# A build-time list scheduler: due times from cumulative TensorE time, SBUF merges counted on a shared port, accumulating transfers assumed to land later

## The chip, the cores and the metric

The kernel runs on one core of a Trainium2 chip. The metric is the device time of one execution in microseconds (us); the number to compare is the median of several executions. A core has five engines that the text names as the profile does: PE (TensorE, matrix products; PEld is its weight load), DVE (VectorE), ACT (ScalarE), POOL (GpSimd) and SP (SyncE, which here only issues transfers). SBUF is the on-chip working memory, PSUM the small memory that PE writes its products to, in banks.

## The reference

An attention block without softmax feeds a mixture of four experts, all in float32:

```python
# q, k, v: (8 batches, 8 heads, 576, 64)
kv  = einsum('bhsd,bhse->bhde', k, v)
out = einsum('bhsd,bhde->bhse', q, kv)
out = out / sqrt(mean(out * out, axis=-1) + 1e-6) * g_norm
x   = out as (4608, 512)                       # N x D
p   = domain_probs / (domain_probs.sum(-1) + 1e-9)
y   = 0
for e in range(4):                             # w1[e]: 512 x 1024, w2[e]: 1024 x 512
    y += p[:, e] * (maximum(x @ w1[e], 0) @ w2[e])
```

## The kernel before

**Tiling.** The 4608 rows of x are nine chunks of 512: one per batch, and a ninth that collects the last 64 rows of every batch. There are 36 steps, s = 9 e + c for expert e and chunk c. A step's `up` makes the hidden layer (x @ w1, ReLU), and its `down` multiplies by w2 and adds the result into the output in DRAM. Both replace eight block products by seven (the scheme of Strassen in the form of Winograd), in `up` on two levels. That saves PE time and adds many sums and differences of blocks in SBUF, which go through `combine` (line 371) and may run on DVE or on POOL, whichever is free.

**Three kinds of steps.** Step 0 has plain products in `up_plain`. Steps 1 to 7 are "mixed": the batch's attention, the two-level `up`, and a `down` with five one-level products per half plus one group, (4, 2), on two levels in `down_deep`. Steps 8 to 34 are "deep": two-level `up` and `down_deep` with four groups. Step 35 is a one-level `down`. The weights of expert e+1 are loaded, and their sums formed, while steps 8, 17 and 26 run: these are the three hand-overs. At a hand-over some forms are made by `subtract_from`: ACT copies a block with the sign turned (line 432), then a transfer from POOL's queue adds DRAM data into it (line 438).

**Merging.** `result` gives each step two accumulators (`acc`, of kind `big`) and the functions `merge` and `send`. `merge` scales by the probability and writes or adds into the accumulator. The first one into a cell is an ACT copy with scale (line 1130). The others are `scalar_tensor_tensor` on DVE (line 1137). In the one-level `down` a merge reads PSUM; in `down_deep` it reads SBUF, where the products have been put together. So in the mixed steps 1 to 7 four merges per step read SBUF on DVE, 28 in all; in the deep steps all SBUF merges are fresh and run on ACT. `send` writes the accumulator out. For expert 0 and at the last step it is a plain transfer from SP's queue (line 1155), otherwise an accumulating transfer from POOL's queue (line 1153). The accumulator's buffer is free when the transfer has landed.

**The order is planned when the kernel is built.** Every operation is added to a `Plan` with a key (its step plus a fraction), a cost by engine, and its dependencies. `Plan.layout` is a list scheduler: it walks through simulated time, and an engine that is free picks an operation which is ready by the plan's clock, within a reach of keys (0.7 for PE, 0.9 for DVE, ACT and POOL). PE and SP take the first ready one in key order. DVE, ACT and POOL take the ready one with the earliest due time. The engines' instruction streams are then issued in the planned order, and each instruction waits for semaphores where its data are not there. The plan also picks the buffers (31 of kind `big`, and two more once the attention is over), so a plan that thinks a buffer free too early makes an instruction wait at the head of its engine's queue.

**Due times.** An operation's own due time is its key times `STEP` (44 us), plus `LATE` (20 us) if it does not run on PE. Going backwards, each operation's due time is then lowered to that of every operation that needs it, less its own cost and a gap of 0.06 or 0.3 us. So `LATE` counts only for operations that lead to no PE work.

**The port.** Operations with `port=True` exclude each other in the plan: `combine` and `add` set it. When the program is written out, a POOL operation with the flag also gets a real dependency on the last such DVE operation before it in the order.

**Landing.** An operation with `kb` that is not on SP is an accumulating transfer: its cost of 1.0 us is followed by 9.0 us for 512 KB and 5.5 us for anything smaller (the sends) until its buffer counts as free, and 0.3 us more.

Of the kernel before, what the change touches and what calls it, by code (L numbers as in the profile page):

```python
# [2 lines left out]

# [31 lines left out]
class Plan:  # L35
# [13 lines left out]

    SPARE = {"big": 6, "small": 3, "xf": 3}  # L50
    FORMS = 9.0
    STEP, LATE = 44.0, 20.0
    SLOW = 6.8

    def __init__(self):
# [27 lines left out]
    def layout(self, slots, later, idle, idle_banks, idle_until):  # L83
# [9 lines left out]
        todo = {e: [] for e in self.REACH}  # L93
# [3 lines left out]
                todo[e].append(op)  # L97
        for e in todo:
            todo[e].sort(key=lambda o: (o.key, o.n))
        for op in self.ops:  # L100
            op.due = op.key * self.STEP + (0.0 if "PE" in op.cost else self.LATE)
        for op in reversed(self.ops):
            for d in op.deps:
                cross = self.SAME if op.cost.keys() == d.cost.keys() else self.CROSS
# [2 lines left out]
        bus, port = 3.8, 0.0  # L107
# [28 lines left out]
        while left:  # L136
# [4 lines left out]
            for eng in todo:  # L141
                if busy[eng] > t:
                    continue
                pending = todo[eng]
                while pending and pending[0].start is not None:
                    pending.pop(0)
                if not pending:
                    continue
                reach = pending[0].key + self.REACH[eng]
                best = None  # L150
                for op in pending:
                    if op.key > reach:
                        break
                    if op.start is not None:
                        continue
                    if best is not None and op.due >= best.due:
                        continue
                    when = ready(op, eng)
                    if when is None:
                        continue  # L160
                    if when > t:
                        heapq.heappush(wake, when)
                        continue
                    best = op
                    if eng in ("PE", "SP"):
                        break
                if best is not None:
                    op = best
                    op.start, op.eng = t, eng
                    if eng == "SP":  # L170
                        busy[eng] = t + op.cost[eng]
                        bus = max(bus, t + 1.5) + op.kb / 215.0
                        op.end = bus + 0.5
                        lanes = lanes[1:] + [op.end]
                    else:
                        op.end = busy[eng] = t + op.cost[eng]
                        if op.kb:
                            op.end += 9.0 if op.kb == 512 else 5.5
                    if op.port:
                        port = op.end  # L180
                        heapq.heappush(wake, port)
                    for b in op.outs:
                        if b.kind is not None and b.slot is None:
                            free[b.kind].sort()
                            b.slot = free[b.kind].pop(0)[1]
                            b.ap = slots[b.kind][b.slot]
                    for b in op.bufs:
                        b.left -= 1
                        if b.left == 0 and b.kind is not None:
                            end = max(o.end for o in [op] + b.readers + b.writers) + self.CROSS  # L190
                            free[b.kind].append((end, b.slot))
                            live[b.kind] -= 1
                            ended[b.kind] = max(end, ended.get(b.kind, 0.0))
                            for rule in [r for r in later if not any(live.get(k) for k in r[0])]:
                                later.remove(rule)
                                end = max(ended[k] for k in rule[0])
                                for ap in rule[2]:
                                    free.setdefault(rule[1], []).append((end, len(slots[rule[1]])))
                                    slots[rule[1]].append(ap)
                                heapq.heappush(wake, end)  # L200
                    heapq.heappush(wake, busy[eng])
                    heapq.heappush(wake, op.end + self.SAME)
                    heapq.heappush(wake, op.end + self.CROSS)
                    order.append(op)
                    left -= 1
                    moved = True
                if eng == "PE" and busy[eng] <= t and 1.6 <= t and front < idle_until:
                    kind, spare = next((
                        (k, f) for k in idle_banks for f in free[k] if f[0] <= t
                    ), (None, None))  # L210
                    if spare is not None:
                        took = 0.43 if t < self.SLOW else 0.23
                        op = Op(front, {"PE": took}, None, (), (), 0, False)
                        op.start, op.eng, op.end = t, eng, t + took
                        op.fn = lambda eng, bank=slots[kind][spare[1]]: idle(bank)
                        busy[eng] = op.end
                        free[kind].remove(spare)
                        free[kind].append((op.end, spare[1]))
                        heapq.heappush(wake, op.end)
                        order.append(op)  # L220
                        moved = True
# [13 lines left out]
def kernel(  # L235
# [105 lines left out]
    def pe(products, columns, passes=2):  # L341
        return {"PE": passes * products * (0.0025 + columns / 1200.0) + 0.003}
# [745 lines left out]
    def result(s, e, c, base):  # L1088
# [6 lines left out]
        acc = [Buf("big", f"acc{s}_{j}") for j in range(2)]  # L1095
# [12 lines left out]
        def cell(i, half=None):  # L1108
            at = (i % 2) * DM
            if half is None:  # L1110
                return acc[i // 2].ap[:, at:at + DM]
            return acc[i // 2].ap[:, at + half * HN:at + (half + 1) * HN]
# [6 lines left out]
                        128, reads=[summed[c, i]], also=[part[i, 0], part[i, 1]],  # L1119
                    )  # L1120

        def merge(key, src, ap, i, half, fresh):

            def prob():
                return p_all[:, c * NR + i, e:e + 1]

            if fresh and not again:
                plan.add(
                    key, {"ACT": 0.48},
                    lambda eng: nc.scalar.activation(  # L1130
                        out=cell(i, half), in_=ap(), func=ACT.Copy, scale=prob()),
                    reads=[probs] + src, parts=[acc[i // 2]], writes=[part[i, half]],
                )
            else:
                plan.add(
                    key, {"DVE": 0.5},
                    lambda eng: nc.vector.scalar_tensor_tensor(  # L1137
                        out=cell(i, half), in0=ap(), scalar=prob(), in1=cell(i, half),
                        op0=ALU.mult, op1=ALU.add,
                    ),  # L1140
                    reads=[probs, part[i, half]] + src, parts=[part[i, half]],
                    holds=[acc[i // 2]],
                )

        def send(key, i):
# [15 lines left out]
            )  # L1161

        return merge, send

    def down(s, e, c, mixed=False):
# [47 lines left out]
    def down_deep(s, e, c, groups=((1, 6), (7, 5), (4, 2), (3,)), base=None, h=None, merge=None, send=None):  # L1213
# [5 lines left out]
        if not mixed:  # L1219
            h = hidden.pop(s)  # L1220
            base = s + 1.2
            merge, send = result(s, e, c, base)
        prods, half = {}, {}
        for i, group in enumerate(groups):
            n = len(group)
            at = base + 2 * i / 7
# [32 lines left out]
            for j, mm in enumerate(ORDER):  # L1259
                key = at + n * j / 49  # L1260
                ps = bank[{2: 2, 5: 5, 3: 5}.get(mm, 1)]

                def product(eng, group=group, mm=mm, ps=ps, forms=forms):
# [11 lines left out]
                op = plan.add(  # L1275
                    key, pe(2 * n, P), product,
                    reads=[b for m in group for b in (w2q[e][m][mm][0], forms[m][mm][0])]
                    + ([ps] if mm == 2 else []),
                    **{"parts" if mm == 2 else "writes": [ps]},
                    after=(inner_last[-2:-1] or primed) if mm == 1 else seeds if mm == 5 else (),  # L1280
                )
# [43 lines left out]
            key = at + n / 7  # L1325

            def whole(m):
                pair, o = prods[m]
                return pair.ap[:, o * NT:(o + 1) * NT]
# [10 lines left out]
            def out_(m, th, dh):  # L1340

                for b in range(2):
                    merge(
                        key - 0.2, [half[m], prods[m][0]],
                        lambda b=b: whole(m)[:, b * HN:(b + 1) * HN], 2 * th + b, dh, not mixed,
                    )

            if mixed:
# [133 lines left out]
```

## Time and profile before

| | us |
|---|---|
| median of 4 runs | 1691.43 |
| lowest and highest of them | 1689.82, 1693.16 |
| the profiled execution, whole | 1693.94 |
| its span, first to last instruction | 1692.2 |
| PE busy in the span | 1678.5 (99%) |
| DVE, ACT, POOL busy | 1252.6 (74%), 985.0 (58%), 733.2 (43%) |
| mean granted PE clock | 0.999 |

A group of instructions is named by line, engine, operation and the tiles it writes and reads; `big<-big,p_all` means that a `big` buffer is written from a `big` buffer and the probabilities. "q" after an engine's name is its queue or sequencer: SPq L377 is a transfer issued from SP. "A <- B: 2.6, 1, 2.6" in the view of waits says that A's engine stood still until B had ended: total us, times, longest. A busy PE counts from the first to the last of its pipelined matmuls, so a half-speed clock shows as busy.

### The profile page before, as it was taken

Reading aid. Unit: us, or ns where it says so; the run is one execution under the profiler, and the core shown is the slowest. Engines: PE = TensorE matmul, PEld = TensorE weight load, DVE = VectorE, ACT = ScalarE, POOL = GpSimd, SP = SyncE. Lnnn points to the kernel's source line nnn. Section 1 sums busy time; section 2 is a strip of 40 time slices with the busy share of each in tenths; the row PEclk is TensorE's granted clock in tenths of the full one; section 3 lists DMA queues with packets and bytes.
Section 4 is the critical chain, followed back from the end, with each engine's and each line's share of the span. In section 5 each row is a group of like instructions: output and inputs, shape, how many; then the busy total and the mean of one; then the engine's idle time right before and its main releaser. Section 6 shows DMA issues by size and latency. Waiting matters only on the chain.

```text
span 1692.2 us, 66409 instructions
## 1 busy us (share of the span) xinstructions
PE 1678.5 (99%) x29030; PEld 1574.1 (93%) x29030; DVE 1252.6 (74%) x2054; ACT 985.0 (58%) x2405; POOL 733.2 (43%) x663
## 2 busy tenths in 40 slices
PE   9999999999999999999999999999999999999998
PEld 6687888888889999999999999999999999999996
DVE  4965675576788678777777887878778877787874
ACT  3454555555455666666665666666666666666662
POOL 3723343434453464333365455334356554343432
PEclk9999999999999999999999999999999999999999
DMA  9865553643556344535477444444478544444442
GB/s 241 227 209 152 174 164 103 183 154 121 185 156 150 114 115 105 121 105 120 132 191 174 114 114 114 114 108 113 110 190 203 123 114 114 114 114 110 119 102 51
DMA packets 172331, 234.27 MB, mean 138 GB/s; under 512 B 61577, under 2 KB 112649, under 8 KB 172041
## 3 DMA queue, kind: packets, MB, share of 16 engines
q1 hardware_dynamic: 148968, 193.32, 37.2%
q0 software_dynamic: 23072, 36.71, 14.8%
q8 instruction: 228, 3.74, 0.9%
q14 instruction: 63, 0.51, 0.1%
HBM read 155.79 MB, written 74.19 MB: 136 GB/s over the span
## 4 chain that ended last, share of the span: by engine, by line
PE 94%; DVE 2%; POOL 1%; DMA 1%; issue 0%; SPq 0%; ACT 0%; ACTq 0%; POOLq 0%; DVEq 0%
PE u L348 44%; PE db L348 31%; PE ab L348 14%; PE ab L708 1%; PE ab L753 1%; PE ab L685 1%; PE ab L735 1%; DVE big L1137 1%; DMA out_dram<-big 1%; POOL rt L593 1%; DVE big L371 1%; DMA small<-in_q_dram 0%; DVE tot L400 0%; POOL xf L371 0%; PE ab L797 0%
## 5 line engine op out<-in xcount | busy, mean ns | idle before, releaser
L371 DVE TENSOR_TENSOR big<-big,big 128x1024 f32<-128x1024 f32 (+1 forms) x524 | 489.3, 949 | 31.8 <-ACT big L951 11.7
L348 PE MATMUL u<-xf,big 128*64 128x128 f32 x6784 | 487.2, 273 | 2.9 <-ACT snap L987 2.8
L348 PEld LDWEIGHTS u<-xf,big 128*64 128x64 f32 x6784 | 393.4, 137 | 8.2 <-ACT snap L987 3.8
L348 PE MATMUL u<-xf,w1y 128*64 128x128 f32 x5304 | 391.8, 273 | 2.1 <-DVE big L995 1.5
L348 PE MATMUL db<-big,big 128*64 128x128 f32 (+1 forms) x4336 | 365.9, 307 | 0.4 <-DVE big L602 0.3
L995 DVE TENSOR_TENSOR big<-u,snap 128x256 f32<-128x256 f32 x464 | 195.0, 421 | 227.8 <-PE u L348 175.7
L371 POOL TENSOR_TENSOR big<-big,big 128x256 f32<-128x256 f32 (+1 forms) x194 | 251.9, 1305 | 257.9 <-DVE big L371 131.4
L348 PEld LDWEIGHTS u<-xf,w1y 128*64 128x64 f32 x5304 | 309.2, 137 | 7.1 <-DVE big L995 1.7
L348 PEld LDWEIGHTS db<-big,big 128*64 128x64 f32 x4336 | 267.0, 137 | 39.4 <-DVE big L602 0.5
L987 ACT ACTIVATE snap<-u 128x256 f32<-128x256 f32 x490 | 188.3, 384 | 168.5 <-PE u L348 131.8
L987 ACT ACTIVATE big<-u 128x256 f32<-128x256 f32 x464 | 178.5, 385 | 103.5 <-PE u L348 80.3
L371 POOL TENSOR_TENSOR big<-big 128x512 f32<-128x512 f32 (+1 forms) x82 | 103.5, 1264 | 120.6 <-DVE big L371 73.6
L1296 ACT ACTIVATE snap<-db 128x256 f32<-128x256 f32 (+1 forms) x230 | 82.7, 359 | 114.4 <-PE db L348 105.5
L951 ACT ACTIVATE big<-big 128x1024 f32<-128x1024 f32 x131 | 137.8, 1052 | 6.3 <-DVE big L371 3.4
L371 DVE TENSOR_TENSOR big<-big 128x512 f32<-128x512 f32 (+1 forms) x130 | 117.5, 911 | 0.5 <-POOL w1y L371 0.5
L1304 DVE TENSOR_TENSOR big<-ab,snap 128x256 f32<-128x256 f32 x170 | 71.7, 422 | 58.9 <-ACT snap L1296 31.0
L987 ACT ACTIVATE u<-u 128x256 f32<-128x256 f32 x245 | 90.8, 371 | 32.4 <-PE u L348 17.7
L1153 POOL DMA_DIRECT2D out_dram<-big x108 | 96.5, 1027 | 27.1 <-ACT big L1130 23.9
L1334 POOL TENSOR_TENSOR big<-big 128x512 f32<-128x512 f32 x24 | 31.2, 1299 | 172.0 <-DVE big L371 170.8
L1130 ACT ACTIVATE big<-big,p_all 128x256 f32<-128x256 f32 x206 | 97.9, 500 | 5.7 <-POOL big L1334 5.3
L348 PE MATMUL db<-kv,big 128*64 128x128 f32 x1360 | 99.1, 273 | 0.0
L348 PE MATMUL ab<-big,big 128*64 128x128 f32 (+1 forms) x1360 | 96.7, 278 | 0.0
(183 smaller groups left out, 2406.9 us busy)
## 6 DMA issues: line engine op xcount, KB each, us to landing
xf<-x SPq DMA_DIRECT2D x108, 512.0 KB, 4.0
out_dram<-big POOLq DMA_DIRECT2D x92, 256.0 KB, 6.4
xf<-x_h SPq DMA_DIRECT2D x81, 256.0 KB, 3.4
xf<-x SPq DMA_DIRECT2D x81, 256.0 KB, 3.9
x<-xf SPq DMA_DIRECT2D x36, 512.0 KB, 4.8
big<-in_moe_w_dram SPq DMA_DIRECT2D x31, 512.0 KB, 5.6
x_h<-big SPq DMA_DIRECT2D x18, 512.0 KB, 4.5
small<-in_q_dram SPq DMA_DIRECT2D x64, 128.0 KB, 4.2
```

Source lines behind the costliest of these rows:

```text
L348: nc.tensor.matmul(out_[cols], lhsT=lhsT[:, cols], rhs=rhs, **kw)
L371: lambda eng: adder(eng).tensor_tensor(out=out_(), in0=a(), in1=b(), op=op),
L593: nc.gpsimd.tensor_tensor(out=rt.ap[0:n, 0:2 * blocks], in0=ss.ap[0:n, 0:2 * blocks], in1=mhalf[0:n, 0:2 * blocks], op=ALU.pow,)
L685: nc.tensor.transpose(bank.ap[:, rs], qt.ap[:, rs], ident[:])
L951: lambda eng: nc.scalar.activation(out=b.ap[:], in_=b.ap[:], func=ACT.Relu),
L987: lambda eng: nc.scalar.activation(out=where(), in_=ps.ap[:, 0:HN], func=ACT.Copy),
L995: lambda eng: nc.vector.tensor_tensor(out=block(whole, a, t), in0=src.ap[:, 0:HN], in1=add_.ap[:], op=ALU.add),
L1130: lambda eng: nc.scalar.activation(out=cell(i, half), in_=ap(), func=ACT.Copy, scale=prob()),
L1153: nc.gpsimd.dma_start(out=dst, in_=cell(i)[parts, :], accum_op=ALU.add)
L1296: lambda eng: nc.scalar.activation(out=where(), in_=group_of(ps.ap), func=ACT.Copy),
L1304: lambda eng: nc.vector.tensor_tensor(out=cell(tq, dq), in0=group_of(src.ap), in1=group_of(add_.ap), op=ALU.add,),
L1334: lambda eng: adder(eng).tensor_tensor(out=whole(to), in0=whole(a), in1=whole(b), op=ALU.add),
```

## The change

Three things change in the plan's model, and nothing in what the kernel computes. First, an operation's due time is no longer its key times 44 us but the sum of the planned PE costs of all PE operations with a smaller key; `LATE` goes from 20 to 30 us. Second, an accumulating transfer that is not of 512 KB counts 8.0 us instead of 5.5 us after its issue cost. Third, the merges of `down_deep` that run on DVE and read SBUF carry the port flag.

```diff
-    STEP, LATE = 44.0, 20.0
+    STEP, LATE = 44.0, 30.0
...
+        keys, begun, spent = [], [], 0.0
+        for op in todo["PE"]:
+            keys.append(op.key)
+            begun.append(spent)
+            spent += op.cost["PE"]
+        begun.append(spent)
         for op in self.ops:
-            op.due = op.key * self.STEP + (0.0 if "PE" in op.cost else self.LATE)
+            at = begun[bisect.bisect_left(keys, op.key)]
+            op.due = at + (0.0 if "PE" in op.cost else self.LATE)
...
                         if op.kb:
-                            op.end += 9.0 if op.kb == 512 else 5.5
+                            op.end += 9.0 if op.kb == 512 else 8.0
...
-        def merge(key, src, ap, i, half, fresh):
+        def merge(key, src, ap, i, half, fresh, from_sbuf=False):
...
-                    holds=[acc[i // 2]],
+                    holds=[acc[i // 2]], port=from_sbuf,
...
                     merge(
                         key - 0.2, [half[m], prods[m][0]],
                         lambda b=b: whole(m)[:, b * HN:(b + 1) * HN], 2 * th + b, dh, not mixed,
+                        True,
                     )
```

The list `todo["PE"]` is sorted by key at that point.

More of the change, by code (lines that the diff above doesn't have):

```diff
@@ L1 @@
+import bisect
 import heapq
```

## The prediction

> **What bounds the kernel now.** I read the page's first section, then a table of windows cut where PE's busy time changes, then what PE waited for, and then the chain of waits and the timeline at the few places that had a wait. A change of order cannot make PE's products cheaper; it can only remove or add time in which PE has nothing ready. So the first question is how much of that there is. The columns of the window table are the length, then busy us (and instructions) of PE, PEld, DVE, ACT and POOL, then clock, DMA share and GB/s.
>
> ```profile
> PE 1678.5 (99%) x29030; PEld 1574.1 (93%) x29030; DVE 1252.6 (74%) x2054; ACT 985.0 (58%) x2405; POOL 733.2 (43%) x663
> ```
>
> ```profile
> 0.00:94.00 94.00, 90.66 (x1274) 60.04 (x1278) 61.49 (x116) 39.93 (x93) 46.66 (x46) 1.00 0.92 249
> 94.00:423.00 329.00, 328.76 (x5265) 276.08 (x5258) 210.51 (x376) 174.15 (x398) 123.31 (x99) 1.00 0.50 151
> 423.00:517.00 94.00, 92.24 (x1423) 81.92 (x1421) 72.82 (x122) 47.63 (x113) 41.88 (x45) 1.00 0.54 171
> 517.00:846.00 329.00, 329.00 (x6030) 328.85 (x6028) 254.72 (x406) 206.48 (x518) 143.56 (x128) 1.00 0.47 119
> 846.00:987.00 141.00, 137.64 (x2479) 136.66 (x2477) 109.03 (x197) 88.26 (x219) 78.33 (x70) 0.99 0.63 154
> 987.00:1269.00 282.00, 282.00 (x5172) 282.00 (x5170) 221.86 (x334) 177.88 (x442) 121.12 (x113) 1.00 0.51 124
> 1269.00:1410.00 141.00, 140.71 (x2564) 139.52 (x2562) 114.27 (x196) 89.36 (x222) 79.62 (x71) 1.00 0.57 140
> 1410.00:1645.00 235.00, 235.00 (x4311) 235.00 (x4307) 185.01 (x277) 146.64 (x371) 90.27 (x87) 1.00 0.48 116
> ```
>
> PE's idle time is 1692.2 - 1678.5 = 13.7 us. The windows place it: 3.34 at the start, 0.24 in the mixed steps, 1.76, 3.36 and 0.29 at the three hand-overs of weights, nothing in the three long deep stretches, and the rest (1645 to the end, 47.20 - 42.47 = 4.73) at the tail, behind the last product. The only prize in the middle is 5.65 us, and what the clock adds to it.
>
> The waits of PE name the two stalls worth having, and the chain at 897 to 911 and the timeline at 502 to 508 say what they hang on.
>
> ```profile
> PE u L348 <- ACT snap L987: 2.8, 2, 2.3
> PE u L348 <- DVE big L995: 1.7, 2, 1.5
> ```
>
> ```profile
> 897.48 11.34 DMA out_dram<-big
> 908.82 0.03 ACTq L432
> ...
> 909.86 0.38 ACT snap L987
> 910.23 0.04 issue
> 910.27 1.09 PE u L348 x8
> ```
>
> An accumulating send left at 897.48 and landed 11.34 us later. ACT's copy at L432 was to overwrite that accumulator and stood at the head of ACT's queue for 2.60 us; the small copies of products (L987) were queued behind it, and PE, whose next product needed one, stood for 2.27 us. The clock paid as well:
>
> ```profile
> 908.00:910.30 2.30, 0.03 (x3) 0.03 (x2) 2.08 (x5) 1.41 (x3) 0.24 (x2) 1.00 1.13 177
> 910.30:913.70 3.40, 3.40 (x32) 3.40 (x34) 0.42 (x1) 1.24 (x4) 2.74 (x3) 0.51 1.08 236
> ```
>
> After the stall PE ran 3.40 us at a clock of 0.51, which loses 3.40 x 0.49 = 1.7 us. The stall's price is 2.27 + 1.7 = 3.97 us.
>
> ```profile
> 502.67 5.05 DVE L1137 SCALAR_TENSOR_TENSOR big<-big,p_all,big 128x256 f32<-128x256 f32 x4
> 504.49 2.54 POOL L371 TENSOR_TENSOR big<-big,big 128x1024 f32<-128x1024 f32 x1
> 508.10 1.09 PE L348 MATMUL u<-xf,w1y 128*64 128x128 f32 x16 [1.46 <-DVE big L995]
> ```
>
> ```profile
> L1137 DVE SCALAR_TENSOR_TENSOR big<-db,p_all,big x38: 472/484/487, 82.4 to 1678.9; 128x256 f32<-128x256 f32 x38
> L1137 DVE SCALAR_TENSOR_TENSOR big<-big,p_all,big x28: 471/832/2589, 187.9 to 507.2; 128x256 f32<-128x256 f32 x28
> ```
>
> Four merges from SBUF ran beside POOL's sums and took 5.05 us together; the sum at L995 that PE needed came behind them on DVE, and PE stood for 1.46 us. The two rows of L1137 (ns, minimum/median/maximum) show the cause: the 38 merges that read PSUM never take over 487 ns, the 28 that read SBUF have a median of 832 and reach 2589. Four such merges at 457.26 took 3.90 us and led the same way to a stall of 0.26 us at 463.70.
>
> **Part 1, merges on the port.** It adds no instruction. POOL operations planned behind a merge gain a wait for it; queued behind that on POOL are other sums and, in the mixed steps, no sends (they are SP's). By the rows, 28 merges take 28.8 us and would take 28 x 0.484 = 13.6 us apart from POOL, so DVE gets back up to 15 us. It is busy 64% of the mixed stretch, so most of that is cover and counts nothing. What reaches the end is 1.46 + 0.26 = 1.72 us. The bounds are 0 (the plan puts another operation late) and 1.96 (a stall of 0.24 us at 312.6, which also has four merges upstream, goes too). I take 1.72, since both stalls hang directly on these merges. The Trainium skill, "SBUF — State Buffer", section "Who interferes with whom", says that a DVE operation with two SBUF inputs and a POOL operation that reads SBUF lock each other out for a whole instruction. That speaks against the change: keeping the two apart would free no engine time in sum, so by it this term would be 0 unless DVE has PSUM work ready meanwhile.
>
> **Part 2, sends land later.** Of the 112 sends from POOL, 48 land later than the old 1.0 + 5.5 = 6.5 us after their start, but only 2 later than the new 9.0. The send that hurt is one of these two, at 11.34. A buffer is planned free 2.5 us later, so ACT's copy would be placed 2.5 us later against a wait of 2.60: 0.1 us is left, and the stall goes with its clock loss, 3.97 us. The bounds are 0 (the copy keeps its place in the order) and 3.97. I take 3.97, since the shift is nearly the whole wait. In the Trainium skill, "TensorE: Matmul & The Clock Gate", section "Why this matters for your kernels", only idle gaps over about 3 us are said to drop the clock. A gap of 2.27 us did it here; by the rule the term would be 2.27.
>
> **Part 3, due times.** By the kernel's `pe` costs a deep step is 49 x 0.44 + 21 x 0.876 + 7 x 0.44 = 43.0 us, against a `STEP` of 44. So in the deep steps the new due times rank operations as the old ones did. A mixed step is 21.5 + 10 x 1.73 + 7 x 0.876 + 10.4 of attention = 55.3 us, and at the start two units of key hold some 19 us of PE work where 88 were counted; there the order of DVE, ACT and POOL changes. The mixed stretch idles 0.24 us in 329, so nothing can be won there. The start idles 3.34, of which 1.35 come before the first product: the bounds are a gain of 2.0 and, with no row for a worse start, a loss of the same 2.0. I take 0.
>
> `LATE` from 20 to 30 moves what leads to no PE work up to 10 us back: in the deep steps the sums of L1334, ACT's merges at L1130 (0.50 us each) and the sends behind them. No DMA changes queue; 26.0 of POOL's waits are sends behind ACT's merges, and the sums queued behind a send on POOL wait with it. Accumulators and product buffers are held that much longer. In the long deep stretches the cover is complete (0 idle). At the hand-overs it isn't: besides the copy at 908.89, two weight loads of SP waited 4.9 us in all for sends to land. A gain is bounded by the stalls that remain (0.48 at 933.1, 0.56 at 977.3, 0.23 at 1320), but there PE waits for copies of products (L987) behind ReLUs and other copies on ACT, all of which lead to PE work, so `LATE` doesn't touch them and I exclude it. The loss is between 0 and one more stall like that at 908, 3.97. I take 1.7: one like the stall at 506.65, and a small one of 0.24.
>
> **The sum.** Against the profiled execution: 1693.94 - 1.72 - 3.97 + 1.7 = 1689.95, 4.0 less. That execution lies 2.51 above the median of the runs, so the median goes to 1691.43 - 4.0 = 1687.4. A change of 0.2%, 3.4 us, is about what a measurement of this kernel can tell from none.
>
> **The rivals.**
>
> *A, stalls removed (my forecast).* For it: both stalls hang on exactly what the plan had wrong. Own range 1683.5 to 1688.0. The lower end takes all of 1.96 + 3.97 with nothing given back (1685.5) and 2.0 from the start. Chance 0.46.
>
> *B, the stalls move.* The send of 11.34 us outlasts the new 9.0 too; if the copy keeps its place the 3.97 stay, and 1.72 - 1.7 leaves 0. Or a wait at 908 goes and one like it comes at another hand-over. Time: 1691.4, or 1688.0 to 1694.8 as a band. For it: after the start PE idles in only eight places, and any new order of DVE, ACT and POOL draws those places anew. Chance 0.28.
>
> *C, slower: the hand-overs starve.* With accumulators planned busy 2.5 us longer and merges up to 10 us later, the buffers for the next expert's weights come free later, and ACT's copies and the loads that fill them wait at the heads of their queues. At 908 the copy waited 2.60 and PE lost 2.27, so only some 0.3 us of slack stood between: whatever a weight form loses beyond that, PE loses, and each time over 2 us the clock's 1.7 comes on top. Two such stalls at 3.97, less the 1.72 of the merges: +6.2, 1697.6. It decides as soon as two of the 48 weight buffers that the hand-overs fill (16 for each of three experts) come over 0.3 us late. Against it: at the third hand-over, with the same work, the whole loss was 0.29 us, so there is room. Chance 0.26.
>
> **How the numbers follow.** Faster 0.46 from A. Same 0.28 from B. Slower 0.26 from C. The range leaves out the top of C and the very bottom of A: 1683.5 to 1697.5.
>
> **What would show it.** In the changed profile the SBUF row of L1137 should have a median near 484 and a maximum under 1 us. No ACT copy at L432 should wait for `out_dram<-big`, the clock should have no dip near 0.5 after the start, and PE's idle time should be near 13.7 - 1.7 - 2.3 + 1.7 = 11.4 us. In the deep steps L1130 and L1334 should run later, with SP's waits for sends at the hand-overs a little longer. A PE idle time over 17 us, gathered in the 100 us behind a hand-over, would make the forecast wrong and C right; a PE idle time of 13 to 14 in new places is B; an idle time that drops only in the first 94 us would mean that I had the wrong part.

## The result, and the profile after

The changed kernel takes 1688.27 us (median of 34 runs) beside 1691.95 us (52 runs of before): a ratio of 0.9978, 95% interval 0.9973 to 0.9983, or 3.7 us less. The forecast was 4.0 us less. The profiled execution went from 1693.94 to 1689.92 us, its span from 1692.2 to 1687.9 us. A few executions that took far longer than the others of their kernel are left out of every ratio.

PE is busy for as long as before, and what changed is its idle time: 13.7 us before, 9.3 us after. The change adds eight lines above the functions that run here, so line 348 is now 356, 371 is 379, 432 is 440, 987 is 995, 1130 is 1138, 1137 is 1145 and 1153 is 1161. First the page's lines, then the table of windows, cut as before:

```profile
span 1687.9 us, 66495 instructions
PE 1678.6 (99%) x29038; PEld 1573.3 (93%) x29038; DVE 1240.2 (73%) x2045; ACT 977.2 (58%) x2405; POOL 716.1 (42%) x672
```

```profile
0.00:94.00 94.00, 90.52 (x1204) 60.07 (x1206) 60.30 (x116) 38.76 (x90) 42.13 (x49) 0.98 0.90 250
94.00:423.00 329.00, 329.00 (x5286) 273.75 (x5282) 202.99 (x368) 172.46 (x397) 111.11 (x96) 1.00 0.48 146
423.00:517.00 94.00, 93.98 (x1456) 83.82 (x1454) 71.76 (x133) 48.24 (x115) 40.24 (x40) 1.00 0.59 183
517.00:846.00 329.00, 328.00 (x6008) 327.58 (x6006) 256.56 (x400) 203.58 (x513) 137.60 (x130) 1.00 0.48 120
846.00:987.00 141.00, 140.97 (x2582) 140.64 (x2580) 113.94 (x203) 91.05 (x227) 72.31 (x69) 1.00 0.64 157
1269.00:1410.00 141.00, 140.97 (x2582) 140.64 (x2580) 111.63 (x197) 89.83 (x227) 76.72 (x67) 1.00 0.59 140
```

Idle time is the first number less the second. Against before the six rows change by +0.14, -0.24, -1.74, +1.00, -3.33 and -0.26, together -4.43 us, close to the 4.3 by which the span is shorter (PE's busy time is 0.1 longer). Every stall that the prediction named is gone, the small ones at 312, 933, 977 and 1320 too, and one is new: PE waited 1.00 us at 536.5 for a load of x.

What PE waited for, the whole list (us in total, times, longest):

```profile
PE ab L716 <- issue: 1.7, 1, 1.7
PE ab L1440 <- POOL ident masks.py:199: 1.4, 1, 1.4
PE u L356 <- DMA xf<-x: 1.0, 1, 1.0
PE ab L821 <- ACT big L769: 0.3, 1, 0.3
```

The merges from SBUF (ns, minimum/median/maximum) run mostly apart from POOL:

```profile
L1145 DVE SCALAR_TENSOR_TENSOR big<-big,p_all,big x28: 470/474/1085, 192.9 to 510.4; 128x256 f32<-128x256 f32 x28
```

Their median fell from 832 to 474 ns, their sum from 28.8 to 14.3 us. No ACT copy at L440 waited for a send. The dip of the clock at 910 is gone, but this execution has another, near the start:

```profile
15.50:17.20 1.70, 0.04 (x1) 0.00 (x0) 0.51 (x2) 0.00 (x0) 1.62 (x2) 1.00 1.03 271
17.20:21.00 3.80, 3.79 (x55) 3.34 (x54) 0.75 (x2) 1.48 (x4) 0.17 (x1) 0.55 1.05 379
```

### The profile page after: what moved, and what is told of

It is laid out like the page before. It is cut to its first block, busy times and chain, and to the rows that moved or that the text cites. A ratio compares the mean times of both kernels' runs of the same rounds, so it can differ in the third digit from the quotient of the medians.

```text
span 1687.9 us, 66495 instructions
## 1 busy us (share of the span) xinstructions
PE 1678.6 (99%) x29038; PEld 1573.3 (93%) x29038; DVE 1240.2 (73%) x2045; ACT 977.2 (58%) x2405; POOL 716.1 (42%) x672
## 4 chain that ended last, share of the span: by engine, by line
PE 99%; DMA 0%; issue 0%; ACT 0%; POOL 0%; DVE 0%; POOLq 0%
PE u L356 47%; PE db L356 32%; PE ab L356 14%; PE ab L716 1%; PE ab L761 1%; PE ab L693 1%; PE ab L743 1%; PE ab L1440 1%; DMA xf<-x 0%; PE ab L697 0%; PE ab L805 0%; PE db L743 0%; PE ab L787 0%; PE ab L821 0%; PE u L743 0%
## 5 line engine op out<-in xcount | busy, mean ns | idle before, releaser
L379 DVE TENSOR_TENSOR big<-big,big 128x1024 f32<-128x1024 f32 (+1 forms) x517 | 500.5, 982 | 43.2 <-ACT big L959 16.7
L356 PE MATMUL u<-xf,big 128*64 128x128 f32 x7072 | 504.8, 273 | 1.0 <-DMA xf<-x 1.0
L356 PEld LDWEIGHTS u<-xf,big 128*64 128x64 f32 x7072 | 409.5, 137 | 5.4 <-DMA xf<-x 1.2
L356 PE MATMUL u<-xf,w1y 128*64 128x128 f32 x5304 | 382.8, 273 | 0.0
L995 ACT ACTIVATE snap<-u 128x256 f32<-128x256 f32 x490 | 187.8, 384 | 194.0 <-PE u L356 138.8
L379 POOL TENSOR_TENSOR big<-big,big 128x256 f32<-128x256 f32 (+1 forms) x156 | 191.5, 1230 | 165.7 <-DVE big L379 75.0
L995 ACT ACTIVATE big<-u 128x256 f32<-128x256 f32 x464 | 177.4, 384 | 89.2 <-PE u L356 68.8
L379 POOL TENSOR_TENSOR big<-big 128x512 f32<-128x512 f32 (+1 forms) x76 | 95.5, 1257 | 161.2 <-DVE big L379 104.8
L1342 POOL TENSOR_TENSOR big<-big 128x512 f32<-128x512 f32 x34 | 44.0, 1294 | 154.0 <-DVE big L379 140.7
L995 ACT ACTIVATE u<-u 128x256 f32<-128x256 f32 x245 | 91.0, 372 | 28.8 <-PE u L356 14.5
L379 DVE TENSOR_TENSOR big<-big 128x512 f32<-128x512 f32 (+1 forms) x121 | 103.3, 857 | 0.4 <-ACT big L1138 0.2
L356 PE MATMUL db<-small,big 128*64 128x128 f32 x1240 | 90.6, 273 | 0.0
L356 PE MATMUL ab<-kv,big 128*64 128x128 f32 x1200 | 83.2, 273 | 0.0
```

The costliest lines, as they stand in the source:

```text
L356: nc.tensor.matmul(out_[cols], lhsT=lhsT[:, cols], rhs=rhs, **kw)
L379: lambda eng: adder(eng).tensor_tensor(out=out_(), in0=a(), in1=b(), op=op),
L995: lambda eng: nc.scalar.activation(out=where(), in_=ps.ap[:, 0:HN], func=ACT.Copy),
L1342: lambda eng: adder(eng).tensor_tensor(out=whole(to), in0=whole(a), in1=whole(b), op=ALU.add),
```

## The experiments

The theory to test was the prediction's: each part acts on the stall it names. Its rival is that any touch of the plan draws the order, and so the stalls, anew. All ratios are to before, timed beside it on the same chip; 0.001 is 1.7 us.

### One mechanism at a time: the order held, one pair of sends, two empty touches

**order_held** keeps before's planned order to the last instruction and adds only the real dependency:

```diff
+                op.apart = from_sbuf            # in merge(); the plan does not see it
...
-            if op.port and op.eng == "DVE":
+            if (op.port or op.apart) and op.eng == "DVE":
                 held = made.ins.name
```

> The order of before, unchanged to the last instruction; only each of the 28 SBUF merges on DVE now holds back the POOL operations after it by a real dependency, as the change does. Theory S (the stalls named in the prediction hang on the contention of merges and POOL): the SBUF row of L1137 comes down from a median of 832 ns to under 600, its total from 28.8 us to under 20, the PE stall at 506.65 from 1.46 to under 0.5 us, and the time by 1 to 2 us (ratio 0.999). The rest, the stall at 908 too, stays. Rival H (the merge was only late in DVE's order, contention or not): the row comes down but the stall stays over 1 us, because POOL's sums that come later now make the same sums on DVE late; ratio 1.000. Rival R (redraw) has no say here, since the order is held.

Measured: 0.9992 (0.9983 to 1.0001). The merges' row, and in the table of windows the first hand-over:

```profile
L1138 DVE SCALAR_TENSOR_TENSOR big<-big,p_all,big x28: 469/481/2581, 188.6 to 505.6; 128x256 f32<-128x256 f32 x28
```

```profile
423.00:517.00 94.00, 93.45 (x1444) 83.07 (x1440) 73.28 (x125) 48.77 (x114) 43.06 (x45) 1.00 0.55 172
```

The median is 481 ns, the sum 21.6 us (over the 20 expected: a merge that starts while POOL is at work is still held, up to 2581 ns). The stalls at 312 and 506 are gone, that at 463 is 0.50. From 94 to 517 us PE idles 0.55 instead of 2.00. So the stall at 506 did hang on the contention, and the mechanism is worth some 1.4 us: the idle time shows it, while the interval of the time just includes nothing. Rival H falls.

**land_one_pair** and the two empty touches:

```diff
-    op.end += 9.0 if op.kb == 512 else 5.5
+    op.end += 9.0 if op.kb == 512 else 8.0 if 18.1 < op.key < 18.3 else 5.5     # land_one_pair
...
-        return {"DVE": 0.155 + 0.00104 * n}
+        return {"DVE": 0.156 + 0.00104 * n}                                     # null_dve_cost
...
-                        bus = max(bus, t + 1.5) + op.kb / 215.0
+                        bus = max(bus, t + 1.5) + op.kb / 214.0                 # null_bus_rate
```

The condition on the key picks two sends of one step, those that filled the accumulator which ACT's copy waited for; the expectation's "each deep step" says more than the edit does.

> Before, with 8.0 us instead of 5.5 us counted for only those sends of each deep step whose key ends in .2 (rows 0 and 1), the kind that held up ACT's copy at 908; nothing else changed. Theory S: the ACT copy at L432 no longer waits 2.60 us for out_dram<-big, the stall of 2.27 us and the clock dip to 0.51 after it are gone, and the span is 3 to 4.5 us less (ratio 0.998), if nothing else comes late. Rival R (redraw: any touch of the plan moves the buffers and the stalls by several us either way): the stall at 908 goes, but PE's idle time in the middle changes elsewhere too, and the time is anywhere within 5 us of before. Rival K (the send of 11.34 us outlasts 9.0 too): the copy still waits over 1 us.

Measured: 0.9997 (0.9988 to 1.0006). The copy no longer waits, PE's idle time from 846 to 987 us falls from 3.36 to 1.09, and no dip follows:

```profile
846.00:987.00 141.00, 139.91 (x2556) 139.18 (x2554) 113.66 (x202) 90.68 (x225) 80.34 (x71) 1.00 0.65 159
```

So the stall went as theory S says, in the trace. In the timed runs it is worth 0.5 us, with an interval from a loss of 1.0 to a gain of 2.0, and not 3 to 4.5. order_held tells why: with the same order at that place, its profiled execution lost 1.54 us there, and the clock stayed at 1.00. First PE's wait, then windows of the stall and of the time behind it:

```profile
PE u L349 <- ACT snap L988: 2.0, 2, 1.5
```

```profile
906.90:908.50 1.60, 0.07 (x2) 0.00 (x0) 1.60 (x4) 1.38 (x3) 0.28 (x2) 1.00 1.13 180
908.50:912.00 3.50, 3.49 (x64) 3.50 (x66) 2.06 (x5) 1.27 (x4) 2.77 (x3) 1.00 1.11 255
```

The difference is the landing of the same send. Its line in the chain of waits (start, length, what), in order_held and in null_dve_cost, one of the two empty touches below:

```profile
896.44 10.61 DMA out_dram<-big
897.63 10.54 DMA out_dram<-big
```

It landed after 11.34 us in before, 10.61 in order_held and 10.54 in null_dve_cost, and PE stood still for 2.27, 1.54 and 1.48: in these three, PE loses what the landing takes longer. The dip is not the rule either. One such dip takes 0.001 off an execution's mean granted clock, and 46 of the 79 executions of before that were timed beside the experiments kept a mean of 1.000. So the profiled execution of before (0.999) had met a bad case, a stall of 2.27 and a dip on top.

> Before, with DVE's planned cost raised by 0.001 us per operation (0.155 to 0.156) and nothing else: a change with no reason behind it. Theory S: what the change brought is due to its parts, so an empty touch stays within 1.5 us of before (ratio 0.999 to 1.001), with the stall at 908 or at 506 still there. Rival R: PE's idle time is drawn anew, and the time moves by over 2 us, either way.

> Before, with the planned rate of SP's transfers at 214 KB per us instead of 215 and nothing else, a second empty touch. Theory S: within 1.5 us of before. Rival R: over 2 us away, either way, with stalls at other places; if both empty touches move by more than the change's 3.7 us, the size of the change's gain can't be put down to its reasons.

Measured: 1.0017 (1.0008 to 1.0025) and 1.005 (1.0037 to 1.0062): 2.9 and 8.5 us slower (2.7 and 9.2 by the medians) from touches with no meaning. null_dve_cost has all the old stalls (1.48 us at 908) and small new ones. null_bus_rate has eleven stalls of 0.48 to 0.79 us from 496 to 517 us; its first hand-over idles 6.45 us:

```profile
423.00:517.00 94.00, 87.55 (x1290) 74.70 (x1288) 68.85 (x114) 44.70 (x103) 40.58 (x49) 1.00 0.55 175
```

Rival R holds, and its spread is larger than the change's gain, though only the second touch moved by more than the 3.7 us that its expectation set as the mark.

### Each part alone

Each is the diff's own part put into before: the port flag (port_alone), 8.0 us for all sends (land_alone), the due times with `LATE` 20 (due_alone), `LATE` 30 with the old due times (late_alone).

> Before with the port flag on the 28 SBUF merges in the plan (part 1 of the change) and nothing else. Theory S (parts act on the stalls they name): the SBUF row of L1137 comes to a median near 480 ns, the stalls at 463 and 506 go, 1.5 to 2 us less than before (ratio 0.999); the stall at 908 stays. Rival R (redraw, as in the empty touches, which moved by +2.9 and +9.2 us): the row comes down all the same, but PE's stalls after 100 us fall elsewhere and the time lies anywhere from -4 to +10 us.

Measured: 1.0018 (1.0009 to 1.0027), 3.0 us slower. The merges are cured (their row first), and PE waits for loads of x instead (its waits behind):

```profile
L1137 DVE SCALAR_TENSOR_TENSOR big<-big,p_all,big x28: 471/480/2239, 188.4 to 510.7; 128x256 f32<-128x256 f32 x28
```

```profile
PE u L348 <- DMA xf<-x: 2.9, 2, 1.5
PE u L348 <- DMA xf<-x_h: 0.9, 1, 0.9
```

These waits are at 500, 511 and 538 us. The cure is the same as in order_held; what differs is the order that the plan makes of it.

> Before with 8.0 us instead of 5.5 us for all sends from POOL (part 2) and nothing else. The sends from POOL begin at 595 us, so up to about 560 us the order must be that of before, with the stalls at 463 and 506 in it. Theory S: the stall at 908 goes; 1 to 4 us less (ratio 0.998 to 0.999), 1 to 1.5 us being what the single pair of sends gave. Rival R: the stall at 908 goes, but the second and third hand-overs get stalls at other places; -4 to +8 us.

Measured: 0.998 (0.9971 to 0.9988), 3.4 us faster, about as much as the whole change. The first 590 us are as before, with the stalls at 463 and 506. After 507 us PE stands still once, for 0.19 us at 1660:

```profile
846.00:987.00 141.00, 141.00 (x2585) 140.82 (x2582) 112.00 (x202) 91.72 (x228) 79.20 (x74) 1.00 0.65 156
1269.00:1410.00 141.00, 141.00 (x2586) 140.82 (x2584) 112.76 (x200) 91.22 (x230) 79.52 (x72) 1.00 0.57 137
```

> Before with due times from cumulative PE time (part 3), LATE kept at 20, no port flag, 5.5 us for sends. The prediction gave this part nothing: within 1.5 us of before (ratio 0.999 to 1.001), with contended merges (median over 700 ns) and some send that holds an ACT copy. Rival D (the due times carry the gain): 3 us or more less than before (ratio 0.998 or lower), with the stalls at 906 to 980 and at 1317 gone. Rival R: anywhere from -4 to +10 us.

Measured: 0.9986 (0.9977 to 0.9995), 2.4 us faster. The first hand-over has no stall left, the second one of 0.48, and the third got worse, from 0.29 to 1.87. The stall at 506 is gone with the merges still contended (24 of them have a median of 832 ns), so another order can hide it too:

```profile
423.00:517.00 94.00, 94.00 (x1460) 84.09 (x1456) 74.93 (x126) 50.09 (x116) 42.02 (x48) 1.00 0.57 179
1269.00:1410.00 141.00, 139.13 (x2536) 138.11 (x2534) 114.45 (x198) 88.34 (x225) 77.85 (x66) 1.00 0.54 135
```

The start, where the prediction looked for this part, has the idle time of before (3.28 beside 3.34). Both hold a stop of PE at about 15 us that no order explains (last section), 1.36 here and 0.27 in before. Without it 1.9 us are left, beside 2.2 to 3.1 in four executions with before's order at the start (before, order_held, land_one_pair, land_alone): a gain there, if any, is of a few tenths to 1 us and not shown.

> Before with LATE at 30 instead of 20 and nothing else. The prediction made this the loss: 0 to +4 us, with later merges (L1130) and SP's loads and ACT's copies waiting longer for accumulators at the hand-overs. Rival D': LATE carries the gain, -2 us or more, since ACT and DVE are freer for what PE needs. Rival R: anywhere from -4 to +10 us, with stalls in places that have nothing to do with sends or merges.

Measured: 1.0016 (1.0008 to 1.0025), 2.7 us slower, by one stall at the first hand-over and the dip behind it. The chain of waits (start, length, what), and the window after the stall:

```profile
499.72 1.33 PE u L348 x17
501.05 4.40 DMA xf<-x_h
505.45 0.14 issue
505.58 0.66 PE u L348 x8
```

```profile
506.50:509.90 3.40, 3.40 (x37) 3.40 (x35) 3.40 (x8) 1.28 (x4) 0.00 (x0) 0.50 1.09 349
```

A load of x stood 5.9 us in SP's queue until PE had read the buffer it overwrites, and then took 4.40 us to land, 4.13 of which PE waited. The loss is of the size forecast and at a hand-over, but not by an accumulator held longer. At the second hand-over this order idles 0.45 us where before idles 3.36, with the landing times of before in its plan: that the stall at 908 goes is by itself no proof of part 2.

Alone, the four parts give +3.0, -3.4, -2.4 and +2.7: -0.1 in sum, where the change gave -3.7.

### The whole, less one part

> The changed kernel without the port flag on the merges; the other parts stay. Theory N (the parts don't add up, each order is drawn anew at the first hand-over): the SBUF merges are contended again (median over 650 ns), and the time is within -1 to +6 us of the changed kernel; the part that alone cost 3.0 us isn't worth a loss of 3.0 here. Rival Sum (parts add up as measured alone: port +3.0, sends -3.4, due times -2.4, LATE +2.7): without the port flag 3 us less than the changed kernel, so 1685.3 beside 1688.3, ratio to before 0.996.

Measured: 1.0011 (1.0002 to 1.002), 5.6 us slower than the changed kernel, by the very stall of late_alone (here at 503.5, with a dip to 0.51 as well):

```profile
PE u L356 <- DMA xf<-x_h: 3.6, 1, 3.6
```

> The changed kernel with the sends at 5.5 us again. Theory N: up to about 590 us, before the first send from POOL, it is the changed kernel; behind it, over 30 sends land after their planned 6.5 us, and at least one makes an ACT copy, a DVE sum or an SP load wait at the second or third hand-over; 0 to +3 us on the changed kernel (ratio to before 0.998 to 1.000). Rival Sum: the part was worth -3.4 us alone, so +3.4 here: the whole gain is gone, ratio 1.000. Rival U (the plan is simply better with free buffers): as fast as the changed kernel or faster, 0.997 to 0.998.

Measured: 0.9987 (0.9977 to 0.9996), 1.5 us slower than the changed kernel, though the two intervals overlap and this one reaches rival U's 0.998. The waits that the part is meant to prevent are back, and stalls of 0.64 us at 906 and 1.00 us at 1286 with them, each at the end of a chain in which an ACT operation waited for a send that landed after 9.13 and 9.63 us. Two rows of waits:

```profile
DVE big L1312 <- DMA out_dram<-big: 4.9, 2, 3.0
ACT big L1304 <- DMA out_dram<-big: 3.1, 2, 2.0
```

> The changed kernel with LATE at 20. Rival Sum: LATE cost 2.7 us alone, so 2.7 us less than the changed kernel, ratio 0.996. Theory N: LATE at 30 is what lets the port flag be had at the first hand-over (the port alone made loads of xf late between 497 and 540 us), so without it stalls on xf or on DVE come back between 480 and 600 us; +2 to +12 us on the changed kernel (ratio 0.999 to 1.005).

Measured: 1.0035 (1.0022 to 1.0047), 9.6 us slower than the changed kernel. The first hand-over idles 6.15 us in a row of small stalls, as in null_bus_rate:

```profile
423.00:517.00 94.00, 87.85 (x1296) 74.88 (x1292) 70.75 (x120) 45.54 (x105) 37.64 (x42) 1.00 0.57 174
```

Theory N (the parts don't add up) holds in all three, in after_no_land by the waits more than by the time, and rival Sum is wrong by 8.6, 1.9 and 12.3 us. No run takes the due times out of the changed kernel, so what they are worth there is not known. `LATE` 30, a loss alone, is worth 9.6 us in the company of the port flag and the due times; the port flag, a loss alone, is worth 5.6.

One thing holds in every order. Five runs count 8.0 us for all sends (land_alone, the changed kernel, after_no_port, after_late20 and land_and_held of the next section): PE idles 0.00 to 0.06 us in their second and third hand-over together (846 to 987 and 1269 to 1410 us), and neither ACT nor DVE waits for a send there. In the other nine PE idles 0.9 to 4.6 us there, and in each of them ACT or DVE waits for a send at least once. So at these two hand-overs part 2 is no lucky draw. Before 595 us, where the first send from POOL starts, it can't act, and from 423 to 846 us PE's idle time is 1.02 us in the changed kernel and anything from 0.00 to 7.2 in the others: there the order is drawn anew.

### A version that beats both

The two touches that did what they name, with nothing else: 8.0 us for the sends, and order_held's dependency.

> The two touches that acted on what they name, put together: before with 8.0 us for the sends (which alone left no PE stall between 507 and 1660 us) and the order of the first 590 us held, with the real dependency on the SBUF merges instead of the port flag in the plan (which alone took the stall at 506 away). No due times, no LATE. Theory S': the stalls at 312, 463 and 506 sum to 0.5 us instead of 2.0, none later; 1 to 1.6 us less than the sends alone, 1686.5 to 1687.0, ratio to before 0.997, faster than the changed kernel by 1 to 2 us. Rival: POOL's added waits make a sum late somewhere in the mixed steps and the time is that of the sends alone, 1688, ratio 0.998.

Measured: 1686.03 us, 0.9966 (0.9954 to 0.9979), 5.8 us less than before; the intervals of this and of the change overlap by 0.0006 only, and its five executions (1685.68 to 1686.47) all lie below the fastest of the changed kernel's 34 (1686.73). PE's list of waits has no stall over 0.5 us after the start:

```profile
PE ab L709 <- issue: 1.5, 1, 1.5
PE ab L1434 <- POOL ident masks.py:199: 1.4, 1, 1.4
PE u L349 <- DVE big L996: 0.5, 1, 0.5
```

## Why the prediction was right, and where only its sum was

**Part 1, 1.72 us.** The mechanism is shown with the order held: idle time 1.45 us less, the time by 1.4 (-0.2 to 2.9). In detail the small stalls changed places: the one at 463 grew from 0.26 to 0.50 us, and the one at 312, which the working kept for its upper bound, went. The step that lacked something is the bound "0, the plan puts another operation late": as a change of the plan alone the part costs 3.0 us, so its bounds should have gone below nothing. By the rule of the Trainium skill, "SBUF — State Buffer", section "Who interferes with whom", as the prediction read it, the term would have been 0; the rows decide for 1.4, since the sum at L995 no longer stood behind a blocked merge. That a merge is locked out while POOL works is what the rows show too: one that meets a running POOL operation still takes up to 2581 ns. Whether a merge locks POOL out in the same way, no row here shows.

**Part 2, 3.97 us.** The mechanism is shown (land_one_pair, after_no_land from the other side, and the five orders against nine), but the term was mis-sized. It priced one execution's stall and its dip, 2.27 + 1.7; two other executions with before's stall at that place (order_held, null_dve_cost) lost 1.54 and 1.48 and had no dip. The working held the clue: it took 3.97 off a profiled execution that lay 2.51 above the median, and then took the 2.51 off again, though the dip and the long stall were most of that excess. For the median the term was about 1.5 by these two traces.

**The remaining stalls, excluded.** The prediction said that `LATE` doesn't touch the 1.3 us at 933, 977 and 1320. It doesn't, but part 2 did: with 8.0 us for all sends those stalls went as well. That makes 2.8 out of 1.5, inside the interval of land_alone's 3.4 (2.0 to 4.9).

**Part 3, due times: 0, in truth -2.4 alone.** The step that failed is to conclude no change from "in the deep steps the new due times rank operations as the old ones did", with bounds taken from the start only. The gain came at the first and second hand-over, and the third lost. The runs don't tell whether ranks changed in the deep steps or whether the new order of the earlier steps was carried on into them.

**`LATE`: +1.7, measured +2.7 alone.** Size and place are right; the cause is a load of x behind its own buffer, not an accumulator.

**The given-back 1.7.** One stall of 1.00 us for a load of x at 536 is what came in its place.

**The sum.** The total, -4.0, was met at -3.7, but that close a match is luck. By place, the second and third hand-over gave 2.9 us (2.92 idle in order_held, 0.06 after) where 3.97 was forecast. The mixed steps and the first hand-over, up to 846 us, gave 1.0 (2.00 idle before, 1.02 after), where 1.72 was forecast and 1.7 given back elsewhere. Two wrong sizes cancelled: the stall at 908 was priced some 2.4 too high, and the small stalls beside it, counted as nothing, went too. Of the signs that the prediction named, the merges came as said (a maximum of 1085 ns and not under 1 us) and no copy waited for a send, but PE's idle time fell to 9.3 us and not 11.4, and SP's waits for sends at the second hand-over went from 4.9 us to none where longer ones were expected. Rival B's sentence, that a new order draws the stalls anew, was the stronger statement for the first hand-over; for the second and third part 2's reason was. The empty touches (+2.9, +8.5) and the parts taken out (+1.5 to +9.6) say that an order of this planner is good for several us either way. That the change's order was a good one could not be read from the profile of before. Rival C's place, the hand-overs, was right: that is where the bad orders idled, most of them at or just behind the first, null_dve_cost at the second and third (4.6 us in sum). Why the first reacts so strongly was not settled: the stalls there end on loads of x, on copies and on sums, in another mix for each order.

## What to carry to other kernels

Where a planner writes the order, a reason that is right was worth 1 to 3 us here and a new order several either way, so test a reason with the order held, or look whether its effect shows in every order, and size up the redraw with an empty touch before crediting a part; parts measured alone need not add up even in sign. A stall read from one profiled execution is a sample: if that execution lies above the median, its worst stall is the first suspect, and its price must not be taken off twice. A mis-stated landing time hurts most at the head of an in-order queue: the copy that waited 2.6 us for its buffer cost PE its next product, because that product's copy was queued behind.

## What the runs showed of the hardware

A merge from SBUF that starts while a POOL operation runs is held until that operation ends. In before, order_held and the changed kernel 37 merges took over 0.52 us; each began inside a POOL operation and ended 0.28 or 0.29 us after it. One of the changed kernel (start, length, what):

```profile
460.04 2.36 POOL L379 TENSOR_TENSOR big<-big,big 128x1024 f32<-128x1024 f32 x1 [1.49 <-PE db L356]
461.59 1.08 DVE L1145 SCALAR_TENSOR_TENSOR big<-big,p_all,big 128x256 f32<-128x256 f32 x1
```

PE stops at about 15 us in 12 of the 14 profiled executions, one matmul before the end of a group, with nothing that the profile shows to wait for: 0.27 us before, 1.67 after, 1.11 in order_held and 1.87 in null_bus_rate, with the same instructions up to there in before, order_held and null_bus_rate. It isn't the order's doing, and adds over 1 us of scatter to any single execution.

The clock's dip does not follow from the length of a stall alone. Stalls of 4.13, 3.59, 2.27 and 1.67 us were followed by some 3.4 us at about half speed; stalls of 1.90 and 1.87 us near the start, and of 1.54 and 1.52 later, by none. What decides it, these runs don't show. The two longest had one in every execution, as far as the mean granted clock tells: none of the 11 executions of late_alone and of the 10 of after_no_port kept a mean of 1.000, where 46 of the 79 of before did. The Trainium skill, "TensorE: Matmul & The Clock Gate", section "Why this matters for your kernels", puts the limit at gaps of about 3 us; here 1.67 us was enough once.
